# Block sums of a seven-product matmul: two VectorE adds and one accumulating DMA in place of one add and two DMAs, with four smaller moves

## Chip, cores and metric

The kernel runs on one core of a Trainium2 chip. The metric is device time in microseconds (us) of one execution; lower is better. Engine names follow the profile: PE is TensorE's matmuls, PEld its weight loads, DVE is VectorE, ACT is ScalarE, POOL is GpSimd, SP is SyncE.

## The reference, cut

```python
def _attn_ref(x):                       # x: (8, 3008, 256) float32
    X = np.fft.fft(x, axis=1)
    X = np.fft.fft(X, axis=2)
    return X.real.astype(np.float32)

def _moe_ref(x, w_in, w_out):           # x: (24064, 256), w_in: (256, 2048), w_out: (2048, 256)
    h = x @ w_in
    g = h * np.cos(h)
    return (g @ w_out).astype(np.float32)
```

## The kernel before

A batch of tokens is folded (16 VectorE operations on the input, the "folds") and goes through a small DFT by matmuls. Then 47 tiles of 256 token columns pass 8 steps each, 376 steps in all. A step does this:

- `mlp1_even`: matmuls of the even part of h into a PSUM bank `hp`; ACT keeps it, times -2, in `pt`.
- `mlp1_odd`: adds the odd part to `hp`. ACT copies `hp` to h, VectorE makes the mirrored half `pt + hp`, and `act_chain` computes h * cos(h) over 1024 columns, which are the four blocks A0 to A3 of 256 columns: ACT, VectorE, ACT, VectorE, each needing the one before.
- `mlp2`: `g @ w_out` of two blocks by two as seven products instead of eight. For that it needs the sums A0+A3, A0+A2+A3 and A0+A1+A2+A3. It runs four steps after its `mlp1_odd` (`LAG = 4`).

After eight steps `combine` adds the products up, and VectorE transposes the result. `pin` keeps instructions in the order of the program; those without it are placed by the scheduler, so an edit can also move neighbours.

The sums before: one VectorE add (A2+A3), an accumulating DMA that finishes two of them, and a second one that finishes the third from the first one's result. The second DMA of a step is issued one step later:

```python
# mlp1_odd, its end
        h = spool.tile([128, 1280], FP, tag="h", bufs=HB, name="h")
        nc.scalar.copy(out=h[:, 0:512], in_=hp)
        nc.vector.tensor_tensor(out=h[:, 1023:511:-1], in0=pt, in1=hp, op=ALU.add)
        act_chain(h, 1024)
        nc.vector.tensor_tensor(
            out=h[:, 1024:1280], in0=h[:, 768:1024], in1=h[:, 512:768], op=ALU.add
        )
        d = spool.tile([128, 768], FP, tag="d", bufs=3, name="d")
        nc.scalar.copy(
            out=d[:, 0:512].rearrange("p (i c) -> p i c", i=2),
            in_=h[:, 0:256].unsqueeze(1).to_broadcast([128, 2, 256]),
        )
        nc.scalar.copy(out=d[:, 512:768], in_=h[:, 256:512])
        nc.gpsimd.dma_start(out=d[:, 0:512], in_=h[:, 768:1280], accum_op=ALU.add)
        T.g[s] = h
        T.d[s] = d

    def sum_last(T, s):
        d = T.d[s]
        pin(nc.gpsimd.dma_start(out=d[:, 512:768], in_=d[:, 256:512], accum_op=ALU.add))

# mlp2: the seven products
            ("Ma", 0, B11, h[:, 0:256]),
            ("Ma", 1, B21, h[:, 256:512]),
            ("Md", 0, T4, h[:, 512:768]),
            ("Mb", 0, T3, d[:, 0:256]),
            ("Mb", 1, T2, d[:, 256:512]),
            ("Mc", 0, T1, h[:, 1024:1280]),
            ("Mc", 1, B22, d[:, 512:768]),

# the loop over steps i
        ends = i >= LAG and (i - LAG) % 8 == 7
        # ... mlp1_even(i) ...
        if i >= LAG:
            T, s = tile_of(i - LAG)
            mlp2(T, s)                      # combine and transposes after s == 7
        # ... at a tile's end: mlp1_even(i + 1) ...
        for j in range(odd_done, min(even_done, total)):
            mlp1_odd(*tile_of(j))
            odd_done = j + 1
        j = i - 1
        if 0 <= j < total:
            sum_last(*tile_of(j))
```

## Time and profile before

| | before |
|---|---|
| time, median of 2 runs | 2433.97 us (2431.27 to 2436.67) |
| profiled span | 2431.5 us |
| PE busy | 2145.8 us, 88% |
| DVE / ACT busy | 1613.1 / 1573.5 us |
| mean granted TensorE clock | 0.952 |

A busy PE at 88% does not say that matmuls run at their best: after a stall the same matmul takes longer (four of line 648: 1.91 us at 1010 us, behind a stall, and 1.03 us at 1026 us, below). So look at the spacing of the starts. In the undisturbed stretch from 1016 to 1027 us the f32 matmul instructions start 0.215 us apart, and one step takes 4.97 us; 376 times that is about 1870 us.

From the page of the kernel before: the span, busy times by engine, and the chain of waits that ended last, first by engine and then by line.

```profile
span 2431.5 us, 27284 instructions
PE 2145.8 (88%) x9540; PEld 1734.1 (71%) x9540; DVE 1613.1 (66%) x2184; ACT 1573.5 (65%) x2446; POOL 680.1 (28%) x790
...
PE 57%; DMA 17%; DVE 11%; ACT 7%; issue 5%; POOL 2%; DVEq 0%; SPq 0%; POOLq 0%; ACTq 0%
DMA d<-d 15%; PE hp L648 10%; PE Mc L719 10%; PE hp L615 10%; PE Ma L719 8%; PE Mb L719 7%; PE Md L719 4%; DVE h L692 4%; ACT r L689 3%; PE hp L627 2%; PE db L377 2%; DVE r L686 2%; POOL d L671 2%; PE da L377 2%; DVE C L754 1%
```

The list of TensorE's waits, kernel before (who waited for whom: us in total, times, longest). `d<-d` is the second DMA, `d<-h` the first; line 719 is the one line that issues all seven products.

```profile
PE Mc L719 <- DMA d<-d: 195.2, 93, 7.1
PE Mb L377 <- issue: 20.4, 1, 20.4
PE hp L615 <- DVE h L660: 12.9, 7, 2.6
...
PE hp L648 <- ACT pt L637: 6.5, 11, 1.0
```

One wait holds two thirds of TensorE's idle time (2431.5 - 2145.8 = 285.7 us), about twice per tile. This is what one looks like, in TensorE's timeline (start, duration, what; an entry joins x like instructions):

```profile
1003.34 0.59 PE L719 MATMUL Mc<-h,T_118 128*128 128x256 f32 x2
1009.47 1.22 PE L719 MATMUL Mc<-d,w_88 128*128 128x256 f32 x2 [5.53 <-DMA d<-d]
1010.48 1.91 PE L648 MATMUL hp<-Ir,Ws 127*128 127x256 f32 x4
...
1026.35 1.03 PE L648 MATMUL hp<-Ir,Ws 127*128 127x256 f32 x4
```

The last product of the step waits 5.53 us. Then four matmuls of line 648 take 1.91 us, where the same four take 1.03 us at 1026: the stall is paid a second time, in a halved clock (the trace grants 0.5 of the clock from 1009.0 to 1012.4 us).

And this is why d is late: POOL's timeline, kernel before.

```profile
1020.54 0.85 POOL L671 DMA_DIRECT2D d<-h  x1 [4.99 <-ACT d L670]
1021.08 1.19 POOL L677 DMA_DIRECT2D d<-d  x1
1027.44 0.85 POOL L671 DMA_DIRECT2D d<-h  x1 [5.17 <-PE hp L648]
1027.98 1.19 POOL L677 DMA_DIRECT2D d<-d  x1
```

The `d<-d` at 1021.08 belongs to the step before. That of the step whose first DMA went out at 1020.54 is the one at 1027.98: it stands in POOL's queue behind the next step's first DMA, which waited for the next step's whole chain. It landed at 1031.51. Over all steps the median from the first issue to the landing of the second is 10.9 us, though the two take only 3.3 and 3.5 us from issue to landing. The page's DMA issues (KB each, median us from issue to landing):

```profile
d<-h POOLq DMA_DIRECT2D x376, 256.0 KB, 3.3
d<-d POOLq DMA_DIRECT2D x376, 128.0 KB, 3.5
```

### The profile page before, as it was taken

Reading aid. Unit: us, or ns where it says so; the run is one execution under the profiler, and the core shown is the slowest. Engines: PE = TensorE matmul, PEld = TensorE weight load, DVE = VectorE, ACT = ScalarE, POOL = GpSimd, SP = SyncE. Lnnn points to the kernel's source line nnn. Section 1 sums busy time; section 2 is a strip of 40 time slices with the busy share of each in tenths; the row PEclk is TensorE's granted clock in tenths of the full one; section 3 lists DMA queues with packets and bytes.
Section 4 is the critical chain, followed back from the end, with each engine's and each line's share of the span. In section 5 each row is a group of like instructions: output and inputs, shape, how many; then the busy total and the mean of one; then the engine's idle time right before and its main releaser. Section 6 shows DMA issues by size and latency. Waiting matters only on the chain.

```text
span 2431.5 us, 27284 instructions
## 1 busy us (share of the span) xinstructions
PE 2145.8 (88%) x9540; PEld 1734.1 (71%) x9540; DVE 1613.1 (66%) x2184; ACT 1573.5 (65%) x2446; POOL 680.1 (28%) x790
## 2 busy tenths in 40 slices
PE   5778998989998898889998799988999889998987
PEld 2557787767777777767777677777777777877765
DVE  3576675766668666676567766677566866666655
ACT  1556676666766666666676666676567666676755
POOL 1222332233322332322232222222223222232322
PEclk8888998999999999999999999999999999999999
DMA  9834454444544454444544445445444444444434
GB/s 203 90 64 94 81 102 76 72 98 82 102 74 74 97 103 77 78 81 91 100 79 77 98 72 100 72 76 102 84 84 80 77 80 71 71 82 81 74 61 78
DMA packets 266969, 209.19 MB, mean 86 GB/s; under 512 B 165186, under 2 KB 213339, under 8 KB 266318
## 3 DMA queue, kind: packets, MB, share of 16 engines
q0 software_dynamic: 111104, 160.53, 38.4%
q1 hardware_dynamic: 153494, 46.83, 9.9%
q8 instruction: 75, 1.23, 0.2%
q10 hardware_dynamic: 2232, 0.07, 0.1%
q14 instruction: 64, 0.52, 0.1%
HBM read 34.71 MB, written 24.78 MB: 24 GB/s over the span
## 4 chain that ended last, share of the span: by engine, by line
PE 57%; DMA 17%; DVE 11%; ACT 7%; issue 5%; POOL 2%; DVEq 0%; SPq 0%; POOLq 0%; ACTq 0%
DMA d<-d 15%; PE hp L648 10%; PE Mc L719 10%; PE hp L615 10%; PE Ma L719 8%; PE Mb L719 7%; PE Md L719 4%; DVE h L692 4%; ACT r L689 3%; PE hp L627 2%; PE db L377 2%; DVE r L686 2%; POOL d L671 2%; PE da L377 2%; DVE C L754 1%
## 5 line engine op out<-in xcount | busy, mean ns | idle before, releaser
L671 POOL DMA_DIRECT2D d<-h x376 | 321.9, 876 | 1572.4 <-ACT d L666 378.1
L686 DVE TENSOR_TENSOR r<-h,r 128x1024 f32<-128x1024 f32 x377 | 456.6, 1220 | 251.4 <-ACT r L683 250.6
L692 DVE SCALAR_TENSOR_TENSOR h<-h,r 128x1024 f32<-128x1024 f32 x377 | 457.4, 1222 | 249.9 <-ACT r L689 245.0
L689 ACT ACTIVATE r<-r,halfpi 128x1024 f32<-128x1024 f32 x377 | 430.5, 1146 | 201.6 <-DVE r L686 201.4
L683 ACT ACTIVATE r<-h 128x1024 int32<-128x1024 f32 x377 | 392.4, 1051 | 105.0 <-DVE h L660 104.9
L677 POOL DMA_DIRECT2D d<-d x376 | 428.5, 1150 | 54.8 <-DMA d<-h 48.3
L615 PE MATMUL hp<-Rr,Wc 128*128 128x256 f32 x1504 | 408.8, 396 | 14.2 <-DVE h L660 12.9
L648 PE MATMUL hp<-Ir,Ws 127*128 127x256 f32 x1504 | 413.3, 401 | 7.5 <-ACT pt L637 6.5
L719 PE MATMUL Mc<-d,w_88 128*128 128x256 f32 x752 | 247.0, 411 | 195.3 <-DMA d<-d 195.2
L660 DVE TENSOR_TENSOR h<-pt,hp 128x512 f32<-128x512 f32 x376 | 252.3, 680 | 226.8 <-ACT h L659 226.3
L719 PE MATMUL Ma<-h,w_88 128*128 128x256 f32 x1504 | 392.6, 384 | 0.0
L659 ACT COPY h<-hp 128x512 f32<-128x512 f32 x376 | 217.6, 581 | 218.7 <-PE hp L648 217.5
L615 PEld LDWEIGHTS hp<-Rr,Wc 128*128 128x128 f32 x1504 | 297.6, 199 | 76.0 <-DVE h L660 24.4
L648 PEld LDWEIGHTS hp<-Ir,Ws 127*128 127x128 f32 x1504 | 292.7, 200 | 65.9 <-ACT pt L637 23.7
L666 ACT COPY d<-h 128x512 f32<-128x512 f32 x376 | 231.8, 617 | 138.2 <-PE Mc L719 95.1
L719 PEld LDWEIGHTS Mc<-d,w_88 128*128 128x128 f32 x752 | 139.6, 197 | 249.1 <-DMA d<-d 234.8
L719 PEld LDWEIGHTS Ma<-h,w_88 128*128 128x128 f32 x1504 | 265.7, 194 | 28.8 <-issue 0.4
L637 ACT ACTIVATE pt<-hp 128x512 f32<-128x512 f32 x376 | 222.7, 592 | 93.7 <-PE hp L627 93.3
L719 PE MATMUL Md<-h,T_121 128*128 128x256 f32 x752 | 224.8, 381 | 5.0 <-DVE T_121 L602 5.0
L719 PE MATMUL Mc<-h,T_118 128*128 128x256 f32 x752 | 224.7, 380 | 1.4 <-DVE C L754 1.3
L719 PE MATMUL Mb<-d,T_120 128*128 128x256 f32 x752 | 224.9, 381 | 0.4 <-DMA d<-h 0.4
L719 PE MATMUL Mb<-d,T_119 128*128 128x256 f32 x752 | 224.6, 380 | 0.0
(351 smaller groups left out, 1863.9 us busy)
## 6 DMA issues: line engine op xcount, KB each, us to landing
d<-h POOLq DMA_DIRECT2D x376, 256.0 KB, 3.3
d<-d POOLq DMA_DIRECT2D x376, 128.0 KB, 3.5
out_dram<-tr SPq DMA_DIRECT2D x252, 64.0 KB
h<-in_moe_w_in_dram SPq DMA_DIRECT2D x4, 512.0 KB
w_88<-in_moe_w_out_dram SPq DMA_DIRECT2D x8, 256.0 KB
out_dram<-tr SPq DMA_DIRECT2D x128, 4.0 KB
out_dram<-tr SPq DMA_DIRECT2D x32, 56.0 KB
out_dram<-tr SPq DMA_DIRECT2D x32, 48.0 KB
```

The costliest lines, as they stand in the source:

```text
L615: nc.tensor.matmul(hp[:, i * TW : (i + 1) * TW], lhsT=Wc[:, f * 128 : (f + 1) * 128], rhs=Rr[:, pos : pos + TW], start=(i == 0), stop=Fals ...
L637: nc.scalar.activation(out=pt, in_=hp, func=AF.Copy, bias=0.0, scale=-2.0)
L648: nc.tensor.matmul(hp[:, i * TW : (i + 1) * TW], lhsT=Ws[0:127, f * 128 : (f + 1) * 128], rhs=Ir[:, pos : pos + TW], start=False, stop=Tru ...
L660: nc.vector.tensor_tensor(out=h[:, 1023:511:-1], in0=pt, in1=hp, op=ALU.add)
L666: nc.scalar.copy(out=d[:, 0:512].rearrange("p (i c) -> p i c", i=2), in_=h[:, 0:256].unsqueeze(1).to_broadcast([128, 2, 256]),)
L671: nc.gpsimd.dma_start(out=d[:, 0:512], in_=h[:, 768:1280], accum_op=ALU.add)
L677: pin(nc.gpsimd.dma_start(out=d[:, 512:768], in_=d[:, 256:512], accum_op=ALU.add))
L683: nc.scalar.activation(out=k, in_=h[:, 0:n], func=AF.Copy, bias=0.25, scale=1.0)
L686: nc.vector.tensor_tensor(out=r[:, 0:n], in0=h[:, 0:n], in1=k, op=ALU.subtract)
L689: nc.scalar.activation(out=r[:, 0:n], in_=r[:, 0:n], func=AF.Sin, bias=halfpi, scale=TWO_PI)
L692: nc.vector.scalar_tensor_tensor(out=h[:, 0:n], in0=h[:, 0:n], scalar=TWO_PI, in1=r[:, 0:n], op0=ALU.mult, op1=ALU.mult,)
L719: nc.tensor.matmul(T.M[bank][:, half * TW : (half + 1) * TW], lhsT=lhsT[:, s], rhs=rhs, start=(s == 0 and half == 0), stop=(s == 7), skip_ ...
```

## The change

The intent: one DMA per step instead of two, so that d is ready sooner; less work in the combine; and more slack for the chain. Cut to its core:

```diff
-        h = spool.tile([128, 1280], FP, tag="h", bufs=HB, name="h")
+        h = spool.tile([128, 1536], FP, tag="h", bufs=HB, name="h")
+        A = [h[:, i * TW : (i + 1) * TW] for i in range(6)]
 ...
-        nc.vector.tensor_tensor(
-            out=h[:, 1024:1280], in0=h[:, 768:1024], in1=h[:, 512:768], op=ALU.add
-        )
-        d = spool.tile([128, 768], FP, tag="d", bufs=3, name="d")
-        nc.scalar.copy(  # h[:, 0:256] twice -> d[:, 0:512]
-        nc.scalar.copy(out=d[:, 512:768], in_=h[:, 256:512])
-        nc.gpsimd.dma_start(out=d[:, 0:512], in_=h[:, 768:1280], accum_op=ALU.add)
+        nc.vector.tensor_tensor(out=A[5], in0=A[3], in1=A[2], op=ALU.add)
+        nc.vector.tensor_tensor(out=A[4], in0=A[0], in1=A[5], op=ALU.add)
+        d = spool.tile([128, 512], FP, tag="d", bufs=DB, name="d")      # DB = 4
+        nc.scalar.copy(out=d, in_=h[:, 0:512])
+        nc.gpsimd.dma_start(out=d, in_=h[:, 768:1280], accum_op=ALU.add)
-    def sum_last(T, s): ...            # and its call in the loop
 ... mlp2: d is read by the fifth and the seventh product
+        for n, (bank, half, lhsT, rhs) in enumerate(parts):
+            if n == 3 and between is not None:
+                between()               # the odd matmuls of step i, except at a tile's end
 ... combine: three copies and seven adds of 256 columns become
+        nc.scalar.copy(out=X[:, 1280:1536], in_=T.M["Ma"][:, 0:TW])
+        for o, a, b in (
+            (Xb[:, 0:5:4], twice(5), blocks(T.M["Mb"])),      # 512 columns
+            (Xb[:, 1:3], twice(4), blocks(T.M["Mc"])),        # 512
+            (Xb[:, 3], Xb[:, 2], T.M["Mc"][:, 0:TW]),         # 256
+            (Xb[:, 1:3], Xb[:, 1:3], blocks(T.M["Md"])),      # 512
 ... the transposes go into turn(T), called at the end of the following step
+        if i >= LAG and (i - LAG) % 8 == 0 and i > LAG:
+            turn(done)
```

The signs of the weight sums follow the new combine. TensorE's instructions are the same in number and shape.

More of the change, by code (lines that the diff above doesn't have):

```diff
@@ L31 @@
 HB = 5
+DB = 4
 def _dft_consts():
@@ L446, in dft_first @@
     def dft_first(xb, **kw):
-        x9 = spool.tile([128, 768], FP, tag="ms", bufs=1, name="x9")[0:9, 0:RUN]
-        lt = spool.tile([128, 2048], BF, tag="C", bufs=1, name="lt")[0:9, 0:RUN]
+        x9 = spool.tile([128, 1536], FP, tag="C", bufs=1, name="x9")[0:9, 0:RUN]
+        lt = spool.tile([128, 1024], BF, tag="ob", bufs=2, name="lt")[0:9, 0:RUN]
         low, high = ring_writers(x9, 0, 0)
@@ L520, in limb_ext @@
         rx = X1[:, 0:HALF]
-        limb = spool.tile([128, 2048], BF, tag="C", bufs=1, name="lx")[0:NB, 0:HALF]
+        limb = spool.tile([128, 3072], BF, tag="C", bufs=1, name="lx")[0:NB, 0:HALF]
         pin(nc.vector.tensor_copy(out=limb, in_=rx))
@@ L558, in fold_ext @@
         n = RUN + 1
-        XA = spool.tile([128, 768], FP, tag="ms", bufs=1, name="XA")[0:NB]
-        XG = spool.tile([128, 1024], FP, tag="C", bufs=1, name="XG")[0:NB]
+        XA = spool.tile([128, 1536], FP, tag="C", bufs=1, name="XA")[0:NB]
+        XG = XA[:, 768:1536]
         def tt(**kw):
@@ L593 @@
     SUMS = (
-        (T1, B11, B12, ALU.subtract),
-        (T2, B22, T1, ALU.add),
-        (T3, B22, B12, ALU.subtract),
-        (T4, T2, B21, ALU.subtract),
+        (T1, B11, 1.0, B12, ALU.subtract),
+        (T2, T1, -1.0, B22, ALU.subtract),
+        (T3, B22, 1.0, B12, ALU.subtract),
+        (T4, T2, -1.0, B21, ALU.subtract),
     )
     def sum_weights(n):
-        o, a, b, op = SUMS[n]
-        pin(nc.vector.tensor_tensor(out=o, in0=a, in1=b, op=op))
+        o, a, sign, b, op = SUMS[n]
+        pin(
+            nc.vector.scalar_tensor_tensor(
+                out=o, in0=a, scalar=sign, in1=b, op0=ALU.mult, op1=op
+            )
+        )
     class Tile:
@@ L661, in mlp1_odd @@
         act_chain(h, 1024)
-        nc.vector.tensor_tensor(
-            out=h[:, 1024:1280], in0=h[:, 768:1024], in1=h[:, 512:768], op=ALU.add
-        )
-        d = spool.tile([128, 768], FP, tag="d", bufs=3, name="d")
-        nc.scalar.copy(
-            out=d[:, 0:512].rearrange("p (i c) -> p i c", i=2),
-            in_=h[:, 0:256].unsqueeze(1).to_broadcast([128, 2, 256]),
-        )
-        nc.scalar.copy(out=d[:, 512:768], in_=h[:, 256:512])
-        nc.gpsimd.dma_start(out=d[:, 0:512], in_=h[:, 768:1280], accum_op=ALU.add)
-        T.g[s] = h
+        nc.vector.tensor_tensor(out=A[5], in0=A[3], in1=A[2], op=ALU.add)
[3 more added lines that the diff above has]
+        nc.gpsimd.dma_start(out=d, in_=h[:, 768:1280], accum_op=ALU.add)
+        T.g[s] = A
         T.d[s] = d
-    def sum_last(T, s):
-        d = T.d[s]
-        pin(nc.gpsimd.dma_start(out=d[:, 512:768], in_=d[:, 256:512], accum_op=ALU.add))
     def act_chain(h, n):
@@ L699, in act_chain, with mlp2 @@
         )
-    def mlp2(T, s):
+    def mlp2(T, s, between=None):
         if s == 0:
@@ L707, in mlp2 @@
             }
-        h, d = T.g.pop(s), T.d.pop(s)
-        for bank, half, lhsT, rhs in (
-            ("Ma", 0, B11, h[:, 0:256]),
-            ("Ma", 1, B21, h[:, 256:512]),
-            ("Md", 0, T4, h[:, 512:768]),
-            ("Mb", 0, T3, d[:, 0:256]),
-            ("Mb", 1, T2, d[:, 256:512]),
-            ("Mc", 0, T1, h[:, 1024:1280]),
-            ("Mc", 1, B22, d[:, 512:768]),
-        ):
+        A, d = T.g.pop(s), T.d.pop(s)
+        parts = (
+            ("Ma", 0, B11, A[0]),
+            ("Mb", 0, B21, A[1]),
+            ("Mb", 1, T2, A[4]),
+            ("Mc", 0, T1, A[5]),
+            ("Mc", 1, T3, d[:, 0:256]),
+            ("Md", 1, T4, A[2]),
+            ("Md", 0, B22, d[:, 256:512]),
+        )
+        for n, (bank, half, lhsT, rhs) in enumerate(parts):
+            if n == 3 and between is not None:
+                between()
             pin(
@@ L722, in mlp2 @@
                     rhs=rhs,
-                    start=(s == 0 and half == 0),
+                    start=(s == 0 and n in (0, 1, 3, 5)),
                     stop=(s == 7),
@@ L731, in combine, with blocks, twice, turn @@
     def combine(T):
-        m1, m2 = T.M["Ma"][:, 0:256], T.M["Ma"][:, 256:512]
-        m7, m6 = T.M["Mb"][:, 0:256], T.M["Mb"][:, 256:512]
-        m5, m3 = T.M["Mc"][:, 0:256], T.M["Mc"][:, 256:512]
-        m4 = T.M["Md"][:, 0:256]
-        ms = spool.tile([128, 768], FP, tag="ms", bufs=1, name="ms")
-        c1, c4, c3 = ms[:, 0:256], ms[:, 256:512], ms[:, 512:768]
-        nc.scalar.copy(out=c1, in_=m1)
-        nc.scalar.copy(out=c4, in_=m4)
-        nc.scalar.copy(out=c3, in_=m3)
-        C = spool.tile([128, 1024], FP, tag="C", bufs=1, name="C")
-        C11, C12, C21, C22 = (C[:, i * TW : (i + 1) * TW] for i in range(4))
-        for o, a, b, op in (
-            (C11, c1, m2, ALU.add),
-            (C22, c1, m6, ALU.subtract),
-            (C21, C22, m7, ALU.add),
-            (C12, C22, m5, ALU.add),
-            (C22, C21, m5, ALU.add),
-            (C12, C12, c3, ALU.add),
-            (C21, C21, c4, ALU.add),
-        ):
-            nc.vector.tensor_tensor(out=o, in0=a, in1=b, op=op)
+        X = spool.tile([128, 1536], FP, tag="C", bufs=1, name="X")
+        nc.scalar.copy(out=X[:, 1280:1536], in_=T.M["Ma"][:, 0:TW])
+        def blocks(t):
+            return t.rearrange("p (i c) -> p i c", c=TW)
+        def twice(i):
+            return X[:, i * TW : (i + 1) * TW].unsqueeze(1).to_broadcast([128, 2, TW])
+        Xb = blocks(X)
+        for o, a, b in (
[3 more added lines that the diff above has]
+            (Xb[:, 1:3], Xb[:, 1:3], blocks(T.M["Md"])),
+        ):
+            nc.vector.tensor_tensor(out=o, in0=a, in1=b, op=ALU.add)
+        T.X = X
+    def turn(T):
+        C = T.X
         for sg in range(2):
@@ L816, in middle_tokens @@
         h = spool.tile([128, 6 * ND], FP, tag="xl0", bufs=1, name="h")
-        e = spool.tile([128, n], FP, tag="em", bufs=1, name="em")
+        e = spool.tile([128, 6 * ND], FP, tag="xl1", bufs=1, name="em")[:, 0:n]
         ev = e.rearrange("p (f b) -> p f b", b=NB)
@@ L939, with odd @@
             even_done = i + 1
+        def odd():
+            nonlocal odd_done
+            while odd_done < even_done:
+                mlp1_odd(*tile_of(odd_done))
+                odd_done += 1
         if i >= LAG:
             T, s = tile_of(i - LAG)
-            mlp2(T, s)
+            mlp2(T, s, None if ends else odd)
             if s == 7:
                 del tiles[T.q]
+                done = T
         if ends and even_done < total:
@@ L947 @@
             even_done += 1
-        starts = i > LAG and (i - LAG) % 8 == 7
-        for j in range(odd_done, min(even_done, total)):
-            mlp1_odd(*tile_of(j))
-            odd_done = j + 1
-        j = i - 1
-        if 0 <= j < total:
-            sum_last(*tile_of(j))
+        odd()
+        if i >= LAG and (i - LAG) % 8 == 0 and i > LAG:
+            turn(done)
+    turn(done)
 _INS = ['x', 'moe_w_in', 'moe_w_out']
```

## The prediction

> **What bounds the kernel now.** TensorE, interrupted. In an undisturbed stretch (timeline, 1016 to 1027 us) one of the 376 steps takes 4.96 us of back-to-back matmuls: f32 instructions start 0.215 us apart. Every TensorE instruction at its undisturbed spacing (0.215; 0.109 for the bf16 ones; 0.316 for the 377-column DFT ones) gives a floor of 2016 us. The other 415 us: about 83 of startup and batch-0 stalls before 240 us, 285 between 240 and 2300 us, some 40 at the two ends.
>
> The list of waits explains the 285: "PE Mc L719 <- DMA d<-d", 195.2 us, 93 times; the chain of waits gives "DMA d<-d" 15%. They recur once or twice per tile, mostly at product step 3 after a tile's end (3.5 to 7 us), more in the fold stages of a new batch. About 75 us is a slowed clock: after a stall, matmuls start 0.43 us apart for some microseconds; mean granted clock 0.952. [...]
>
> Why d is late: the second DMA of step j (d<-d) stands in the POOL queue behind the first of step j+1 (d<-h). At 1020.5 the first goes out; the second only at 1027.98, landing at 1031.5: 11 us for two DMAs of 3.3 and 3.5 us.
>
> **What the change does.**
> - Removes 376 d<-d DMAs and that queueing: d is ready 3.3 us after its one issue, about 7.5 us earlier. On the critical path.
> - ACT: per step 617 + 404 ns of copies become one 128x512 copy, about 600: -158 us; combine -35 us. ACT isn't the limit.
> - VectorE: +1 add of 128x256, 419 ns x 376 = +157 us. Combine: 7 adds (2.92 us) become three of 512 columns (0.68 each, as the h add) and one of 256: 2.46 us, -22 us. Busy 1613 -> about 1748 us.
> - Moves: odd matmuls three products earlier (more slack for the chain); transposes (1.4 us) behind the next chains; d read by products 5 and 7. TensorE work is unchanged.
>
> From odd matmul to d needed: about 20 us mid-tile, 17.5 us at a tile's end. Chain after: 0.58+0.68+1.05+1.22+1.15+1.22+0.84+0.5+3.3 = 10.5 us, some 14 to 16 with interleaved neighbours and combine. So ordinary tiles stop stalling. In fold stages VectorE needs 3.97 + 1.27 + 0.48 = 5.7 us per step against 4.96: it becomes the limit for 12 steps per batch, a new wait of 3 to 6 us for each of 7 batches.
>
> **Sum.** 2016 + 73 startup and batch 0 + 75 main loop (fold stages 35, tile ends and x loads 25, clock 15) + 40 ends = about 2205 us (range 2150 to 2290), 9.4% less. Faster by over 2%: 0.95; within 2%: 0.03; slower: 0.02.
>
> **What would show it.** Right: products' waits on d fall from 195 us to under 60; clock 0.97 or more; VectorE busy 1730 to 1765, ACT 1370 to 1400; DMA landing still near 3.3 us; remaining main-loop stalls cluster in fold stages.
>
> **What would make it wrong.** VectorE, in order at 80% busy, placing folds, transposes or combine ahead of a chain, so that stalls return as waits on d<-h or on hp; longer landings; PSUM waits of the new tile on the wider combine.

What the trace shows is that after the stall of 5.69 us at 1009.5 us the matmuls started 0.43 us apart. 2016 + 73 + 75 + 40 = 2204, put as about 2205 us. The floor of 2016 is counted from the spacings in the trace; the other three terms are estimates, from the losses in the trace of the kernel before (about 83 us before 240 us, 285 in the main loop, some 40 at the ends). In the chain, 0.5 is the estimate for the way from ready inputs to the DMA's issue (0.6 us in the median, kernel before), and "14 to 16" is one for the whole (in the kernel after it is 13.0 us in the median from the end of the odd matmuls to the landing). "In order" is what the trace of the kernel before shows: VectorE's instructions follow one another, and none starts more than 0.09 us before the end of the one before it.

## The result

| | before | after |
|---|---|---|
| time, median of 2 runs | 2433.97 us | 2172.80 us (2172.76 to 2172.84) |
| ratio | | 0.8927 (0.8884 to 0.897) |
| profiled span | 2431.5 us | 2171.1 us |
| PE busy / idle | 2145.8 / 285.7 us | 2071.5 / 99.6 us |
| DVE / ACT busy | 1613.1 / 1573.5 us | 1723.5 / 1461.0 us |
| mean granted clock | 0.952 | 0.988 |

A ratio is the mean time of one kernel's fast runs over that of the other's fast runs of the same rounds, with a 95% interval; so it is not quite the ratio of the medians. The forecast was 2205 us, with a range of 2150 to 2290.

The page of the kernel after, the lines that answer to those of before:

```profile
span 2171.1 us, 26759 instructions
PE 2071.5 (95%) x9540; PEld 1688.2 (78%) x9540; DVE 1723.5 (79%) x2419; ACT 1461.0 (67%) x1976; POOL 353.5 (16%) x414
...
PE 44%; DVE 29%; ACT 19%; issue 5%; DMA 2%; DVEq 0%; SPq 0%; ACTq 0%
DVE h L690 10%; DVE r L684 8%; ACT r L687 8%; PE hp L653 8%; ACT r L681 7%; PE hp L620 7%; PE Md L720 7%; PE Mc L720 6%; PE Mb L720 6%; PE Ma L720 3%; PE db L378 3%; PE da L378 3%; ACT d L672 3%; DVE h L667 2%; PE hp L632 2%
```

TensorE's waits, kernel after (L653 is the odd matmul, L720 a product, L751 the combine):

```profile
PE Mb L378 <- issue: 21.7, 1, 21.7
PE hp L653 <- ACT pt L642: 19.6, 63, 0.9
...
PE Mc L720 <- DVE X L751: 4.7, 4, 1.7
PE Mc L720 <- DVE h L667: 3.5, 1, 3.5
PE Mb L720 <- DVE X L751: 3.3, 3, 1.9
PE Md L720 <- DVE X L751: 1.9, 3, 0.6
...
PE Mc L720 <- DMA d<-h: 1.1, 1, 1.1
```

The wait for d fell from 195.2 us to 1.1 us. POOL's timeline in the kernel after has one issue per step, and the landing took 3.3 us in the median as before (the last line, from the page's DMA issues):

```profile
1006.72 0.85 POOL L673 DMA_DIRECT2D d<-h  x1 [4.55 <-ACT r L681]
1012.11 0.84 POOL L673 DMA_DIRECT2D d<-h  x1 [4.54 <-ACT r L681]
1017.03 0.84 POOL L673 DMA_DIRECT2D d<-h  x1 [4.08 <-PE hp L653]
...
d<-h POOLq DMA_DIRECT2D x376, 256.0 KB, 3.3
```

The 260.4 us of span split into two parts that the busy line gives directly: 186.1 us less idle TensorE (285.7 - 99.6), and 74.3 us less busy time for the same 9540 matmul instructions (2145.8 - 2071.5). By the estimate that follows, the second part is mostly the clock. By the trace's clock record TensorE was busy for 155.9 us at half clock in the kernel before and for 17.0 us in the kernel after; half of the difference, 69 us, is an estimate of what the slow clock cost (at half clock the matmuls behind the stall at 1009.5 us start 0.43 us apart in place of 0.215, so half of that time is lost). After 240 us there are 31 stretches of half clock before, and two after, both behind 2070 us. I looked at what follows each TensorE stall of over 1 us after 240 us in the kernel before. (A stall is counted here from where the next matmul would have started at the undisturbed spacing; the profile's idle time is about 0.16 us shorter.) With a stall of 3.8 us or more, at least half of the next ten or so matmuls started 0.3 to 0.6 us apart, in 13 of 13 cases; from 2.7 to 3.6 us in 16 of 19; from 1.0 to 2.7 us in one of 31 (2.03 us, three of six). The kernel after has one stall of over 2.1 us in that stretch.

### The profile page after: what moved, and what is told of

Same layout as the page of the kernel before. It is cut to its first block, busy times and chain, and to the rows that moved or that the text cites. A ratio compares the mean times of both kernels' runs of the same rounds, so it can differ in the third digit from the quotient of the medians.

```text
span 2171.1 us, 26759 instructions
## 1 busy us (share of the span) xinstructions
PE 2071.5 (95%) x9540; PEld 1688.2 (78%) x9540; DVE 1723.5 (79%) x2419; ACT 1461.0 (67%) x1976; POOL 353.5 (16%) x414
## 3 DMA queue, kind: packets, MB, share of 16 engines
q1 hardware_dynamic: 153494, 46.83, 10.6%
## 4 chain that ended last, share of the span: by engine, by line
PE 44%; DVE 29%; ACT 19%; issue 5%; DMA 2%; DVEq 0%; SPq 0%; ACTq 0%
DVE h L690 10%; DVE r L684 8%; ACT r L687 8%; PE hp L653 8%; ACT r L681 7%; PE hp L620 7%; PE Md L720 7%; PE Mc L720 6%; PE Mb L720 6%; PE Ma L720 3%; PE db L378 3%; PE da L378 3%; ACT d L672 3%; DVE h L667 2%; PE hp L632 2%
## 5 line engine op out<-in xcount | busy, mean ns | idle before, releaser
L653 PE MATMUL hp<-Ir,Ws 127*128 127x256 f32 x1504 | 396.1, 389 | 22.4 <-ACT pt L642 19.6
L620 PE MATMUL hp<-Rr,Wc 128*128 128x256 f32 x1504 | 387.1, 380 | 1.7 <-DVE h L667 1.3
L672 ACT COPY d<-h 128x512 f32<-128x512 f32 x376 | 231.8, 617 | 180.9 <-DVE h L690 170.9
L653 PEld LDWEIGHTS hp<-Ir,Ws 127*128 127x128 f32 x1504 | 268.1, 189 | 105.3 <-ACT pt L642 75.6
L620 PEld LDWEIGHTS hp<-Rr,Wc 128*128 128x128 f32 x1504 | 284.7, 190 | 50.1 <-DVE h L667 5.4
L720 PE MATMUL Mc<-h,T_118 128*128 128x256 f32 x752 | 224.6, 380 | 4.7 <-DVE X L751 4.7
L720 PE MATMUL Mc<-d,T_120 128*128 128x256 f32 x752 | 223.4, 379 | 4.6 <-DVE h L667 3.5
L720 PE MATMUL Mb<-h,w_88 128*128 128x256 f32 x752 | 224.4, 380 | 3.3 <-DVE X L751 3.3
L720 PE MATMUL Md<-h,T_121 128*128 128x256 f32 x752 | 224.6, 380 | 2.9 <-DVE X L751 1.9
L720 PE MATMUL Ma<-h,w_88 128*128 128x256 f32 x752 | 225.1, 381 | 0.0
L720 PE MATMUL Mb<-h,T_119 128*128 128x256 f32 x752 | 224.1, 380 | 0.0
L720 PE MATMUL Md<-d,w_88 128*128 128x256 f32 x752 | 224.1, 380 | 0.0
L720 PEld LDWEIGHTS Mc<-h,T_118 128*128 128x128 f32 x752 | 142.9, 191 | 25.7 <-issue 6.3
L720 PEld LDWEIGHTS Mc<-d,T_120 128*128 128x128 f32 x752 | 141.7, 189 | 25.7 <-DVE h L667 3.9
```

Of the source, the lines that this page charges most:

```text
L620: nc.tensor.matmul(hp[:, i * TW : (i + 1) * TW], lhsT=Wc[:, f * 128 : (f + 1) * 128], rhs=Rr[:, pos : pos + TW], start=(i == 0), stop=Fals ...
L653: nc.tensor.matmul(hp[:, i * TW : (i + 1) * TW], lhsT=Ws[0:127, f * 128 : (f + 1) * 128], rhs=Ir[:, pos : pos + TW], start=False, stop=Tru ...
L672: nc.scalar.copy(out=d, in_=h[:, 0:512])
L720: nc.tensor.matmul(T.M[bank][:, half * TW : (half + 1) * TW], lhsT=lhsT[:, s], rhs=rhs, start=(s == 0 and n in (0, 1, 3, 5)), stop=(s == 7 ...
```

## The experiments

All experiments but e2 gave the correct result. Medians; "before" was 2438 to 2440 us in these. A run stands against the kernel before of the same rounds; the kernel after was timed once, on another occasion (2172.8 us, two runs). Its ratio is known to 0.0043 either way, which is 10 us, so I do not call differences to it of under about 10 us firm.

| run | what | time, us | ratio to before |
|---|---|---|---|
| after | the change | 2172.80 | 0.8927 |
| e1_same_step | before, second DMA issued in its own step | 2205.18 | 0.9030 |
| e2_no_second | before, no second DMA (wrong result) | 2176.34 | 0.8910 |
| e3_sums_only | only the new block sums | 2208.04 | 0.9048 |
| e4_dma_back | after, idle DMA from d put back, 3 buffers | 2218.91 | 0.9097 |
| e4b_dma_free | after, idle DMA from h put back, 3 buffers | 2188.28 | 0.8971 |
| e11_db3 | after, 3 d buffers | 2182.00 | 0.8948 |
| e5_odd_late | after, odd matmuls behind the products | 2172.66 | 0.8911 |
| e6_turn_now | after, transposes at once | 2186.39 | 0.8971 |
| e10_dve_more | after, one more VectorE add per step | 2214.77 | 0.9081 |
| e7_fold_even | after, folds spread | 2162.13 | 0.8863 |
| e8_between5 | after, odd matmuls behind the fifth product | 2164.91 | 0.8881 |
| e12_both | e7 and e8 together | 2150.25 | 0.8813 |

My theory: d was late because of the order in POOL's queue, and that is nearly the whole gain. Rival 1: the second DMA's traffic and the ACT work cost the time. Rival 2: the order of odd matmuls, combine and transposes did.

### e1_same_step: only the queue order

```diff
-        nc.gpsimd.dma_start(out=d[:, 0:512], in_=h[:, 768:1280], accum_op=ALU.add)
+        pin(nc.gpsimd.dma_start(out=d[:, 0:512], in_=h[:, 768:1280], accum_op=ALU.add))
         T.g[s] = h
         T.d[s] = d
+        sum_last(T, s)
 ... in the loop
-        j = i - 1
-        if 0 <= j < total:
-            sum_last(*tile_of(j))
```

> The kernel before, with one edit: the second accumulating DMA of a step is issued straight behind its own first one, no longer behind the first one of the next step. All work, DMA bytes and TensorE order stay. Theory (the POOL queue makes d late): d is complete about 7 us after its first issue instead of about 11, the products' waits on d fall from 195 us to under 100, time 2260 to 2340 us. Rival 1 (DMA traffic of the second DMA, or ACT work, is what costs): nothing of it is gone, 2420 to 2445 us. Rival 2 (the order of odd matmuls, combine and transposes is what costs): also 2420 to 2445 us.

Measured: 2205.18 us, ratio 0.9030 (0.8994 to 0.9066), so 90% of the change's gain (0.0970 of 0.1073). That is more than I had expected (2260 to 2340), and both rivals are far off. (The edit also pins the first DMA in its place in the program; e2 below does not, and gains as much.) The median from the first issue to d's completion fell from 10.9 to 6.7 us, and the landing of the second DMA alone from 3.5 to 2.6 us. POOL's timeline of e1, and the page's DMA issues:

```profile
1020.44 0.84 POOL L678 DMA_DIRECT2D d<-d  x1 [4.67 <-DMA d<-h]
1021.02 1.13 POOL L671 DMA_DIRECT2D d<-h  x1
1025.06 0.85 POOL L678 DMA_DIRECT2D d<-d  x1 [2.90 <-DMA d<-h]
1025.64 1.14 POOL L671 DMA_DIRECT2D d<-h  x1
...
d<-h POOLq DMA_DIRECT2D x376, 256.0 KB, 3.5
d<-d POOLq DMA_DIRECT2D x376, 128.0 KB, 2.6
```

POOL now sits and waits for its own first DMA to land, 2.9 us per step in the median. The trace puts this wait on POOL, before the second DMA's issue. It is not free: the next step's `d<-h` stands behind it (it follows 0.58 us after `d<-d` in both pairs above). In 208 of e1's 376 steps the first DMA went out more than 1 us after its inputs were ready (the ends of ACT's copy and VectorE's add), against 13 steps in the kernel before (counts over the two traces). Counted from the ready inputs, d was complete after 8.5 us in the median in place of 11.5, so 3.0 us sooner and not 4.2. TensorE felt little of that here; its wait in e1:

```profile
PE Mc L720 <- DMA d<-d: 30.2, 18, 7.9
```

Of 195.2 us, 30.2 are left. I had sized this gain too small because I took it as a share of the wait. But 64 of the 93 waits in the kernel before were shorter than 3 us, so they can vanish whole, and with them goes the slow clock (0.952 to 0.979).

### e2_no_second: no second DMA, no added VectorE work

```diff
-        j = i - 1
-        if 0 <= j < total:
-            sum_last(*tile_of(j))
```

> The kernel before without the second accumulating DMA at all; the result is wrong on purpose (one of seven products reads an unfinished sum). VectorE gets no added work, ACT keeps its copies. Theory: waits on d fall under 40 us and the time to 2180 to 2240 us: nearly the whole gain of the change without the rest of it. Rival 2 (odd matmuls, combine, transposes): at most a third of the gain, 2340 us or more.

Measured: 2176.34 us, ratio 0.8910 (0.8874 to 0.8946), slightly faster than expected. TensorE's waits in e2; on d there are 1.9 us left:

```profile
PE Mb L377 <- issue: 22.4, 1, 22.4
PE hp L615 <- DVE h L660: 17.1, 22, 2.6
...
PE Mb L719 <- DMA d<-h: 1.9, 2, 1.8
```

The old order, combine and transposes are all still there. So an early d, with nothing paid for it, is worth as much as the whole change. Rival 2 falls as the main cause.

### e3_sums_only: the new block sums without the other parts

```diff
-DB = 4
+DB = 3
 ... combine: seven adds of 256 columns, same algebra
         T.X = X
+        turn(T)                         # transposes straight behind the combine
 ... in the loop
-            mlp2(T, s, None if ends else odd)
+            mlp2(T, s)                  # odd matmuls behind all seven products
```

> The kernel after with the other parts undone: odd matmuls behind all seven products, seven adds of 256 columns in the combine, transposes straight behind the combine, three d buffers. What is left of the change is the block sums (two adds on VectorE, one DMA). Theory: 2185 to 2250 us, at least 70% of the gain of 261 us. Rival 2: 2340 us or more.

Measured: 2208.04 us, ratio 0.9048 (0.9013 to 0.9083), 89% of the gain. It stands 32 us above e2, which differs mainly in not having the added VectorE add, and level with e1. So making A0+A2+A3 on VectorE is by itself no better than issuing the second DMA in its own step. My reading is that it removes a DMA but adds work to an engine that is nearly full in places (e10 below prices such work); no run separates this from the other differences between e3 and e2. The other parts of the change bring the last 35 us.

### e4_dma_back and e4b_dma_free: is the traffic the cost?

Both put back one accumulating DMA of 128 KB per step into a scratch tile that nobody reads; both have three d buffers, to make room (no run shows whether four would have fitted), and both pin the first DMA.

```diff
+    def dma_back(T, s):                 # called for step i - 1, as sum_last was
+        pin(nc.gpsimd.dma_start(out=scr, in_=T.d[s][:, 256:512], accum_op=ALU.add))   # e4
+        pin(nc.gpsimd.dma_start(out=scr, in_=T.g[s][1], accum_op=ALU.add))            # e4b
```

> The kernel after (with three d buffers, to have room) with a second accumulating DMA of 128 KB per step put back, from d into a scratch tile that nobody reads, queued as in the kernel before. Traffic and POOL work of before are back, the wait is not. Theory: 2165 to 2200 us, within 1.5% of the kernel after. Rival 1 (traffic, contention in landing): 2230 us or more, and the first DMA's landing goes above 3.6 us.

> As e4_dma_back (three d buffers, one more accumulating DMA of 128 KB per step into a scratch tile, queued behind the next step's first DMA), but it reads a block of h, of which there are five buffers, so it does not keep d's buffer, which ACT then waited for. Theory (bytes and POOL issues cost nothing here; e4's 46 us were the buffer): 2165 to 2190 us, waits of hp on pt back under 30 us. Rival 1 (traffic costs): 2205 us or more, as e4.

Measured: e4 2218.91 us (0.9097), against the expectation; e4b 2188.28 us (0.8971). The landing of the first DMA stayed at 3.3 us in e4. By its lists of waits, what cost time in e4 was less the traffic than a new reader of d: ACT's copy into d waited for the DMA to let go of the buffer, and behind that copy in ACT's queue stood `pt`, for which the odd matmuls then waited. ACT's list of waits in e4 has

```profile
ACT d L674 <- DMA scr<-d: 49.6, 30, 9.2
```

and TensorE's has

```profile
PE hp L655 <- ACT pt L644: 42.9, 91, 3.0
```

where the kernel after has 19.6 us.

With a source that has spare buffers (e4b), 31 of the 46 us are gone. That source is not quite free either; ACT's list of waits in e4b has

```profile
ACT h L668 <- DMA scr<-h: 14.7, 6, 4.4
```

### e11_db3: the control

```diff
-DB = 4
+DB = 3
```

> The kernel after with three d buffers in place of four, nothing else: the control for e4b_dma_free[...]. If e4b's 15 us are the buffer: 2183 to 2192 us here. If they are the extra DMA's bytes or POOL issues: 2170 to 2178 us here.

Measured: 2182.00 us (0.8948), between the two expectations. By the medians about 9 us of e4b's 15 are the missing fourth buffer, and about 6 us are left for the DMA's bytes, POOL's issues and the hold on h. The intervals of the kernel after, e11 and e4b overlap, so this split is not firm; but rival 1 comes to some 6 us of 261. The fourth buffer is probably a useful part of the change: with three, ACT's copy waits for the products to finish with d (`ACT d L672 <- PE Md L720`: 141.6 us in 152 waits, against 4.2 us in 3 in the kernel after).

### e5_odd_late and e8_between5: where the odd matmuls stand

```diff
-            mlp2(T, s, None if ends else odd)
+            mlp2(T, s)                          # e5
-            if n == 3 and between is not None:
+            if n == 5 and between is not None:  # e8
```

> The kernel after with one part undone: odd matmuls behind all seven products. Of the 35 us by which e3_sums_only is slower than the kernel after, theory gives this part 5 to 20 us: 2178 to 2195 us, waits on d above the 1 us of the kernel after, waits of hp on pt lower. Rival (it is free or harmful because odd matmuls wait for pt sooner): 2160 to 2174 us.

> The kernel after with the odd matmuls between the fifth and sixth product in place of the third and fourth. Theory (early odd matmuls gain nothing because they now wait for pt, 19.6 us in 63 short waits and as much again in waits under 0.3 us, while late ones let d, hp and X be late): the middle place has both small: waits of hp on pt under 10 us, time 2150 to 2166 us. Rival (both places are equal because the gain is elsewhere): 2169 to 2176 us.

Measured: e5 2172.66 us (0.8911), the same as the kernel after; the rival was right. e8 2164.91 us (0.8881, 0.8852 to 0.8910). TensorE's waits of e5:

```profile
PE hp L653 <- ACT pt L642: 16.4, 21, 1.7
PE hp L620 <- DVE h L667: 11.4, 8, 6.3
PE Mc L720 <- DMA d<-h: 10.6, 5, 7.2
...
PE Mc L720 <- DVE X L751: 10.0, 7, 2.5
```

Late odd matmuls let d, hp and X come late again (10.6, 11.4 and 10.0 us). Early ones stand only three products (1.3 us) behind the even part, and ACT has not always made `pt` by then (19.6 us in 63 waits, kernel after). In the kernel after, 238 of the starts of odd matmuls after 240 us come more than 0.02 us later than the undisturbed spacing, 45 us in sum; in e5 it is 67 and 21 us. The two balance. Behind the fifth product (e8) it is 77 and 20 us, with d at 4.6 us and hp at 6.0 us. The listed wait for `pt` fell only to 16.5 us (24 times), not under 10 as expected, and e8's interval overlaps that of the kernel after, so its 8 us are likely but not firm by themselves.

### e6_turn_now: the transposes

```diff
-        if i >= LAG and (i - LAG) % 8 == 0 and i > LAG:
-            turn(done)
 ... in combine
+        turn(T)
```

> The kernel after with one part undone: transposes straight behind the combine. Theory: 1.4 us of VectorE work per tile stand ahead of the next chains again, 5 to 20 us: 2178 to 2195 us, in waits on d and on X. Rival (the slack that the shorter sum chain leaves covers it): 2168 to 2178 us.

Measured: 2186.39 us (0.8971), 14 us slower than the kernel after, as expected in size (its interval, 0.8947 to 0.8996, just overlaps that of the kernel after, and is clear of that of e5 in the same rounds). The losses did not come back as waits on d; they are spread over small waits, and which of them carry it stays open. The moved edit also made the scheduler place other VectorE and ACT instructions differently.

### e10_dve_more: what VectorE work costs now

```diff
         nc.vector.tensor_tensor(out=A[4], in0=A[0], in1=A[5], op=ALU.add)
+        nc.vector.tensor_tensor(out=state["r"][:, 0:256], in0=A[1], in1=A[2], op=ALU.add)
 ... act_chain keeps its tile in state["r"]
```

> The kernel after with one more useless VectorE add of 128x256 per step (0.42 us, 157 us of work in all), written over the spent r tile. Theory (VectorE is full in the fold stages and has room elsewhere): 84 fold steps at 0.42 us are 35 us, plus tile ends: 2205 to 2255 us. If VectorE had room everywhere: under 2185 us. If it were the limit throughout: 2320 us.

Measured: 2214.77 us (0.9081), 42 us more for 157 us of added work (an estimate: 376 adds of the 0.42 us that such an add took in the kernel before). So about a quarter of the added work came through to the time. Busy times of the kernel after by stretch show where: a fold stage of 12 steps, then a stretch without folds (columns: stretch, its length, then busy us and instructions of PE, PEld, DVE, ACT, POOL, then the granted clock, DMA share, GB/s).

```profile
400.60:464.40 63.80, 60.83 (x288) 50.56 (x287) 62.54 (x88) 44.71 (x63) 9.96 (x12) 1.00 0.31 58
...
1260.00:1320.00 60.00, 59.17 (x265) 47.30 (x264) 42.53 (x61) 37.94 (x53) 10.70 (x13) 1.00 0.33 66
```

In this fold stage VectorE is busy 62.54 of 63.80 us and a step takes 5.3 us instead of 4.97; outside it is busy 71% of the time. In the six fold stages from 390 us on, a step takes 5.1 to 5.4 us, and VectorE is busy 92% of the time or more.

### e7_fold_even and e12_both: a faster kernel

```diff
-            at(s0 + 10 + i * 3 // 4, lambda key=key: state["ops"][key]())
+            at(s0 + (10 + i * 9 // 8 if b == 1 else 2 + i * 5 // 3), lambda key=key: state["ops"][key]())
```

> The kernel after with the 16 fold operations of a new batch spread over 25 steps in place of 12. Theory (VectorE is full in the fold stages, and TensorE loses about 22 us in the six main ones): VectorE's demand falls from 5.7 to about 5.0 us per step, most of that loss goes: 2150 to 2164 us. Rival (the loss in those stages is small waits for pt and the like, which have nothing to do with the folds): 2168 to 2176 us.

> The edits of e7_fold_even and e8_between5 together, as a candidate for a faster kernel. Theory: the two losses are at different places, so the gains add: 2135 to 2155 us. If they share slack: no better than the better of the two.

Measured: e7 2162.13 us (0.8863); e12, with the edit of e8 as well, 2150.25 us (0.8813, 0.8785 to 0.8840). Both times are in the expected range and the gains add up. e7's interval (0.8835 to 0.8890) still touches that of the kernel after; e12's lies clear of the kernel after's: it is the fastest correct kernel here, 1.0% below the change by the medians. To see where e7 gains, I summed by how much matmul starts exceed their undisturbed spacing, over the same 25 steps of each of six batches (those that hold the fold operations in both kernels, and the tile ends behind them): 37.9 us in the kernel after, 27.3 us in e7. That is 10.6 us, and the time fell by 10.7 us. In the other steps the two hardly differ (16.5 and 15.5 us). By name, the waits on X (4.7 + 3.3 + 1.9 us) are gone from e7's list. In e8 it is the other way round: 34.9 us, and 9.3 us in the other steps. In e12 both are low: 21.4 and 9.7 us.

## Why the prediction was right

- **The bound: right.** TensorE, held up by d. That wait fell from 195.2 to 1.1 us, and e2 shows that an early d alone is worth the whole difference.
- **The cause, POOL's queue: right, and shown by e1**, which changes little but that order and has 90% of the gain. That d would come about 7.5 us earlier was right too: from the first issue to d's completion the median fell from 10.9 to 3.3 us. Only its share was not stated in the prediction, and I then guessed it too small for e1.
- **The clock: right.** The slow clock cost up to 74 us, by the estimate above 69, against the 75 of the forecast. The clock rose to 0.988; 0.97 or more was forecast. What stalls of each length did here is in the last section.
- **VectorE in the fold stages: right in kind, wrong in form and size.** It is nearly full there (busy 92% or more), and spreading the folds (e7) takes away 10.6 us of TensorE's loss. But the forecast "new wait of 3 to 6 us" per batch did not come: between 240 and 2060 us no stall of the kernel after is over 2.1 us. The loss is spread over many small delays. It sums to some 18 to 25 us over the fold stages of six batches, depending on where a stage is cut, against a forecast of 35 us for seven. (The 37.9 us of the 25 steps hold other losses too: most of it stays when the folds are spread.) The demand per step was put at 5.7 us and is at most the 5.1 to 5.4 us that a step took.
- **Odd matmuls three products earlier, "more slack for the chain": wrong.** e5 shows no gain. The slack was real (waits on d of 1.1 us, against 10.6 in e5), but the wait for `pt` (19.6 us in 63 waits, against 16.4 in 21) took it back; the prediction had not followed that chain.
- **ACT's busy time: mis-sized.** It fell by 112 us, not 193, to 1461.0 us where 1370 to 1400 was forecast. The mean durations that I added up overlap at their ends when copies follow one another closely (the copy at line 666 starts 0.52 us before that at line 670 in the median, though it lasts 0.62 us), so their sum exceeds the busy time. It did not matter, because ACT, 67% busy in the kernel after, is not the limit. VectorE's 1723.5 us is just below the forecast 1730 to 1765.
- **The sum: 32 us too high.** Counted from late matmul starts in the same way, the kernel after loses 64 us in the first 240 us (forecast 73), 61 us from there to 2060 us (75), and 27 us at the two ends (40). For one, the three waits on d of 3.9 to 6.7 us in the first 240 us, which I had mostly kept in the sum, went away too. That the middle term came so close is partly luck: its 15 us of slow clock did not come at all, the folds were put too high, and the late odd matmuls (about 45 us, some of them in the fold stages) were not in it.

Left open: e1 with the later parts of the change (transposes, fourth buffer, wide combine) and without the extra VectorE add might be faster than either kernel. No run tried it.

## What to carry to other kernels

A wait at the head of an engine's queue delayed what stood behind it, on POOL (DMA issues: 10.9 us in the median from a step's first issue to the landing of its second, for two DMAs of 3.3 and 3.5 us) as on ACT (`pt` in e4: 42.9 us of TensorE's waits against 19.6). If a transfer is late, compare its issue with the moment its inputs were ready before paying another engine to replace it: here, moving one issue by one place gave 90% of what the replacement gave. And a TensorE stall of 2.7 us or more was here mostly worth more than its length: slow matmuls followed in 29 of 32 cases in the kernel before.

## What the traces show of stalls and accumulating DMAs

- When a stall slows the matmuls behind it: the edge is not sharp here. In the kernel before, stalls (counted as above) of 2.74 to 3.04 us were already followed by slow matmuls in all five cases, three between 3.47 and 3.59 us were not, and in e1 one of 2.08 us was; from 3.8 us on all were (13 of 13). The shortest stalls with slow matmuls behind them were of 2.0 to 3.0 us in these two runs.
- The time of an accumulating DMA from SBUF to SBUF: here 256 KB took 3.3 us (median) from issue to landing. 128 KB took 3.5 us issued right behind such a one (before), and 2.6 us issued after that one had landed (e1), even though the next 256 KB mostly followed within 1 us.
- What a wait before a DMA's issue costs others: in e1 a DMA issue that waits for an earlier one's landing held POOL for 2.9 us per step in the median and made the next step's first DMA over 1 us late in 208 of 376 steps, at little cost to TensorE (30.2 us of waits on d), while the one-step-later order cost 234 us (before against e1, by medians).
